# The second layer's output product by one step of Strassen's scheme, with its operand through DRAM

## The chip, the cores and the metric

The kernel runs on one core of a Trainium2 chip. The metric is the device time of one execution in microseconds; the median of several runs counts. Beside the runs there is one profiled execution with a trace of every instruction. The engines are TensorE (PE, with its weight loads as PEld), VectorE (DVE), ScalarE (ACT), GpSimd (POOL) and SyncE (SP), whose queue issues all DMAs here.

## The reference

A causal attention with a cumulative bias, then two feed-forward layers. What is touched is the second layer:

```python
def _moe2_ref(x, w_in, w_out):          # x (2304, 512), w_in (512, 2048), w_out (2048, 512)
    h = x @ w_in
    g = h - np.tanh(h)
    return (g @ w_out).astype(np.float32)
```

The weights come as float64 and the products have to be as exact as float32.

## The kernel before

Each operand of a product is held as two float32r parts, a high part `h` and the rest `l`, and each product is three matmuls: high by high, high by low, low by high. ScalarE makes the high part by a copy, VectorE or GpSimd the low one by a subtraction. Weights arrive as float64 words and pass through `Conversion`: a DMA of 512 KB, one ScalarE operation, three VectorE operations on 512 words (lines 88, 89, 91), a ScalarE copy and a GpSimd subtraction.

The stages follow each other: attention with the gate and value products of the first layer (matmuls of 256 and 320 columns at lines 347, 348, 351), the first layer's output product (lines 540 to 559, blocks of 384 tokens), then the second layer. The order on each engine is the order in which the code issues, and SP's queue takes its DMAs in that order too; a DMA whose buffer isn't free holds up those behind it.

The second layer runs over 6 blocks of 384 tokens and, in each, over 16 pieces m of 128 columns of the hidden width. `hmm` makes the tanh product of one (block, m): 12 matmuls of 384 columns into one of two banks (lines 581, 582, 585), then tanh on ScalarE, the subtraction, the copy to the high part and the subtraction of the low part. `outp` adds the piece's share of the output: 9 matmuls of 512 columns (line 605), three token tiles by three parts, into three banks that stay open over the 16 pieces. `outp` of a pair is issued behind `hmm` of the next, so that the tanh chain has a tanh product's time. In the first block the output weights are still being converted, by POOL among others. At the end of a block ScalarE and VectorE copy the three banks out and SP stores them. `ysplit` makes the two parts of the layer's input y, four copies and four subtractions for a block.

## Time and profile before

| | us |
|---|---|
| median of 3 runs | 1157.69 (1157.55 to 1158.14) |
| profiled execution, span | 1156.5 |
| of it: TensorE busy | 1063.0 |
| VectorE busy | 724.9 |
| ScalarE busy | 539.2 |
| GpSimd busy | 391.1 |
| matmuls | 6501 |

The span is the time from the first to the last instruction of the profiled execution; the time of a run has about a microsecond around it. The shares of the span mean little here, since the attention stage is shared among all engines while the two output products and the second layer are not. One has to read the stages apart: the view of stretches gives the busy time of each engine in each, the timeline the distance between instructions, the groups by shape the mean length of an operation. A matmul's printed length contains its way through the array; how many fit into a microsecond is told by start times alone.

### The profile page before, as it was taken

The page shows a single profiled execution, that of the slowest core. Times are in us where ns is not written, and L with a number is a line of the kernel's source. Part 1 is how long each engine was busy: PE and PEld are TensorE (multiplying, and loading weights), DVE is VectorE, ACT ScalarE, POOL GpSimd, SP SyncE. Part 2 cuts the span into 40 slices and gives each one's busy share as a digit, 9 for nine tenths or more (in the row PEclk, how much of TensorE's full clock was granted, in tenths as well). Part 3 has the DMA queues.
Part 4 walks back from the last instruction along what each step waited for, and adds up shares of the span by engine and source line. Part 5 has one row for each costly group of instructions (what it writes and reads, how often), then busy time and mean ns, then how long its engine had stood idle before and what let it go on. Part 6 is the DMA issues. An engine that isn't in the chain of part 4 may idle for free.

```text
span 1156.5 us, 18998 instructions
## 1 busy us (share of the span) xinstructions
PE 1063.0 (92%) x6501; PEld 997.0 (86%) x6501; DVE 724.9 (63%) x1783; ACT 539.2 (47%) x1325; POOL 391.1 (34%) x524
## 2 busy tenths in 40 slices
PE   3457799989999999999899999999999999999998
PEld 2346699989899899898889999997899999999997
DVE  7999967688878788873856677378423233232322
ACT  4565556566666666653434444344323232232322
POOL 6786645466656566651311222023000000000000
PEclk9999999999999999999999999999999999999999
DMA  6556444443433433321746655233000000000000
GB/s 190 163 161 176 115 119 127 135 144 114 132 120 124 120 125 120 119 77 40 231 146 180 185 167 172 71 96 106 28 1 28 1 22 6 1 28 1 28 1 28
DMA packets 64417, 114.11 MB, mean 99 GB/s; under 512 B 7168, under 2 KB 40960, under 8 KB 64320
## 3 DMA queue, kind: packets, MB, share of 16 engines
q1 hardware_dynamic: 64320, 112.90, 31.8%
q8 instruction: 51, 0.84, 0.3%
q14 instruction: 46, 0.38, 0.1%
HBM read 93.92 MB, written 18.95 MB: 98 GB/s over the span
## 4 chain that ended last, share of the span: by engine, by line
PE 72%; DVE 15%; issue 5%; DMA 3%; ACT 3%; SPq 0%; POOL 0%; DVEq 0%; ACTq 0%; POOLq 0%
PE bank L605 15%; PE bank L348 6%; PE bank L347 6%; PE bank L351 6%; PE bank L581 5%; PE bank L582 5%; PE bank L585 5%; PE bank L300 4%; DVE raw L89 4%; PE bank L548 4%; PE bank L549 4%; PE bank L552 4%; PE bank L273 4%; PE bank L223 2%; DMA raw<-in_wo 2%
## 5 line engine op out<-in xcount | busy, mean ns | idle before, releaser
L588 DVE TENSOR_TENSOR th<-bank,th 128x384 f32<-128x384 f32 x96 | 53.5, 557 | 196.2 <-ACT th L587 196.1
L273 PE MATMUL bank<-ident,sp 128*128 128x128 f32 (+1 forms) x480 | 78.6, 273 | 68.8 <-DVE ptl L287 35.2
L286 ACT ACTIVATE pth<-bank 128x320 fp32r<-128x320 f32 (+2 forms) x160 | 69.6, 435 | 146.8 <-PE bank L300 88.1
L587 ACT ACTIVATE th<-bank 128x384 f32<-128x384 f32 x96 | 46.9, 488 | 192.0 <-PE bank L585 192.0
L273 PEld LDWEIGHTS bank<-ident,sp 128*128 128x128 f32 (+1 forms) x480 | 51.8, 143 | 86.6 <-DVE ptl L287 37.7
L243 ACT ACTIVATE sp<-sp,nm 128x576 f32<-128x576 f32 (+2 forms) x160 | 95.9, 599 | 45.0 <-DVE nm L236 44.8
L287 DVE TENSOR_TENSOR ptl<-bank,pth 128x320 fp32r<-128x320 f32 (+2 forms) x160 | 77.6, 485 | 49.0 <-ACT pth L286 33.0
L206 POOL TENSOR_SCALAR_AFFINE_SELECT nb<-nb 128x128 f32<-128x128 f32 x160 | 48.0, 300 | 150.9 <-DVE nb L205 115.1
L592 DVE TENSOR_TENSOR g2l<-th,g2h 128x384 fp32r<-128x384 f32 x96 | 53.6, 558 | 56.7 <-ACT g2h L591 56.7
L591 ACT ACTIVATE g2h<-th 128x384 fp32r<-128x384 f32 x96 | 50.4, 525 | 62.4 <-DVE th L588 62.4
L205 DVE TENSOR_SCALAR nb<-cbc,cumn 128x576 f32<-128x576 f32 (+2 forms) x160 | 76.6, 479 | 2.2 <-DMA cbc<-cum 2.2
L236 DVE CUSTOM_DVE_ANT_0 sp<-bank,nb 128x288 f32<-128x288 f32 (+2 forms) x160 | 75.6, 472 | 1.2 <-POOL nb L206 0.2
L223 PE MATMUL bank<-kh,qs 128*128 128x384 f32 (+1 forms) x192 | 70.7, 373 | 6.0 <-POOL qs L172 6.0
L89 DVE SCALAR_TENSOR_TENSOR raw<-raw 128x512 uint32<-128x512 uint32 x68 | 74.2, 1091 | 2.3
L496 DVE TENSOR_TENSOR gl<-g,gh 128x384 fp32r<-128x384 f32 x72 | 39.6, 556 | 57.3 <-PE bank L552 38.1
L261 DVE TENSOR_SCALAR sp<-sp,r 128x128 f32<-128x128 f32 (+1 forms) x96 | 72.6, 756 | 3.4
L168 POOL TENSOR_TENSOR kl<-kq,kh 128x256 fp32r<-128x256 f32 (+1 forms) x64 | 73.0, 1141 | 3.6 <-ACT kh L167 2.8
L300 PE MATMUL bank<-pth,vs 128*128 128x256 f32 (+1 forms) x224 | 71.2, 335 | 0.6 <-ACT pth L286 0.6
L495 ACT ACTIVATE gh<-g 128x384 fp32r<-128x384 f32 x72 | 37.1, 526 | 71.2 <-PE bank L549 60.8
L96 ACT ACTIVATE tmp<-raw 128x512 f32<-128x512 f32 x68 | 45.5, 669 | 46.6 <-DMA raw<-in_wo 26.8
L300 PE MATMUL bank<-ptl,vs 128*128 128x256 f32 (+1 forms) x224 | 64.7, 309 | 0.1
L91 DVE SCALAR_TENSOR_TENSOR tmp<-tmp,raw 128x512 uint32<-128x512 uint32 x68 | 59.9, 881 | 6.0 <-DVE raw L89 0.5
(588 smaller groups left out, 3405.3 us busy)
## 6 DMA issues: line engine op xcount, KB each, us to landing
kq<-in_kq SPq DMA_DIRECT2D x32, 448.0 KB, 3.6
raw<-in_wo SPq DMA_DIRECT2D x28, 512.0 KB, 3.6
g<-g SPq DMA_DIRECT2D x72, 192.0 KB, 3.4
cbc<-cum SPq DMA_DIRECT2D x32, 288.0 KB, 4.0
kq<-in_kq SPq DMA_DIRECT2D x32, 256.0 KB, 3.5
raw<-in_win SPq DMA_DIRECT2D x16, 512.0 KB, 3.6
g<-gt SPq DMA_DIRECT2D x48, 160.0 KB, 1.8
raw<-in_wg SPq DMA_DIRECT2D x12, 512.0 KB, 4.4
```

What stands on the lines that cost most here:

```text
L89: DVE.scalar_tensor_tensor(out=lo, in0=lo, scalar=29, in1=hi, op0=ALU.logical_shift_right, op1=ALU.bitwise_or)
L168: POOL.tensor_tensor(out=kl, in0=d["k"], in1=kh.bitcast(F), op=ALU.subtract)
L205: DVE.tensor_scalar(out=n, in0=c, scalar1=cumn[:, t, j:j + 1], scalar2=0.0, op0=ALU.add, op1=ALU.min)
L223: PE.matmul(ps, d["qs"][:, o:o + 128], d["kh"][:, c0:c1], start=True, stop=False)
L236: DVE.tensor_tensor_reduce(out=sp[:, c0:c1], in0=ps[:, 0:c1 - c0], in1=e["nb"][:, c0:c1], scale=-0.125, scalar=init, op0=ALU.add, op1=ALU. ...
L243: ACT.activation(out=e["sp"], in_=e["sp"], func=AF.Exp, scale=-1.0, bias=e["m"], accum_out=e["sum"])
L261: DVE.tensor_scalar(out=e["sp"], in0=e["sp"], scalar1=e["r"], scalar2=None, op0=ALU.mult)
L273: PE.transpose(ps[:, j, :], e["sp"][p0:128, c:c + 128], ident[p0:128, p0:128])
L286: ACT.activation(out=ph[:, js, o:o + n], in_=e["tr"], func=AF.Copy)
L287: DVE.tensor_tensor(out=pl[:, js, o:o + n], in0=e["tr"], in1=ph[:, js, o:o + n].bitcast(F), op=ALU.subtract)
L300: PE.matmul(ps[:, o:qw], d["vs"][:, j].rearrange("p a d -> p (a d)"), p[:, slot, o:qw], start=(n == 0 and m == 0), stop=(n == len(jobs) - ...
L605: PE.matmul(acc[t], g[:, t * 128:t * 128 + 128], w, start=(m == 0 and k == 0), stop=(m == M2 - 1 and k == 2))
```

## The change

The second layer falls into two stages. In the first, `hmm` runs alone, over 8 blocks of 288 tokens by 16 pieces (128 units), into eight banks in turn; each unit's g, h minus tanh(h) in float32, is stored to DRAM (`g2scr`). In the second, the output product is made from four quarters of g (token halves by halves of the hidden width) and four quarters of the output weights, by seven products in place of eight (Strassen's scheme in Winograd's form).

The seven weight operands of a pair p of pieces (p and p + 8) are made during the first stage by `PairConversion`: two 512 KB loads, the conversion as before, four GpSimd sums of 256 columns, two ScalarE copies and two GpSimd subtractions for the two parts. Pairs 0 to 2 stay in SBUF; pairs 3 to 7 are stored to DRAM (`w2scr`, 1.84 MB each) and come back over the place of the input weights (`wload`): 3 and 4 in the last block, 5 to 7 in the first steps of the second stage.

The second stage runs over five passes s of tokens (four of 256 in each half, one of 128) and in each over the 8 pairs p; (s, p) is called a step here. `sload` loads the four quarters' pieces of g (0.52 MB, three DMAs, two buffers); `sprep` makes three of the seven operands by a copy and four by sums: two on POOL, two on VectorE, then two ScalarE copies (768 and 1024 elements) for the high and two VectorE subtractions for the low parts, into buffers that are used in turn by every second step. A step has 42 matmuls of 256 columns, in the short pass 21, into seven banks, one for each product. In the last step of a pass `drain` copies product 1 out by ScalarE and adds the others on VectorE, seven additions, and four stores leave. The first layer's stage loses three conversions (from 19 to 16), and the pools are laid out anew. The diff, cut; the conversion's arithmetic is moved into two functions and unchanged:

```diff
+MP = M2 // 2
+ND = 3
+HBLK = 288
+NHB = NT // HBLK
+TB = 256
+DG = 2
+NSB = -(-(NT // 2) // TB)
+OG = {1: 0, 2: 1, 3: 6, 4: 2, 5: 3, 6: 4, 7: 5}
+OW = {1: 2, 2: 0, 3: 1, 4: 6, 5: 3, 6: 4, 7: 5}
+OORD = (1, 2, 6, 7, 5, 4, 3)
...
+    class PairConversion:
...
+            yield start
+            yield second
+            yield join(0)
+            yield join(1)
+            yield self.keep
+            for a in todo[:2]:
+                yield add(*a)
+            yield lambda: self.load(p + 1)
+            yield high(*cuts[0])
+            for a in todo[2:]:
+                yield add(*a)
+            yield low(*cuts[0], False)
+            yield high(*cuts[1])
+            yield low(*cuts[1], True)
...
-        if blk < NBLK:
+        if blk < NHB:
...
-        ps = bank(i % 2, [128, BLK])
+        ps = bank(i % 8, [128, HBLK])
...
-        th = fp.tile([128, BLK], F, tag="th2", name="th2")
+        th = fp.tile([128, HBLK], F, tag="th2", name="th2", bufs=6)
         ACT.activation(out=th, in_=ps, func=AF.Tanh)
         DVE.tensor_tensor(out=th, in0=ps, in1=th, op=ALU.subtract)
-        gh = fp.tile([128, BLK], R, tag="g2h", name="g2h")
-        gl = fp.tile([128, BLK], R, tag="g2l", name="g2l")
-        ACT.activation(out=gh, in_=th, func=AF.Copy)
-        DVE.tensor_tensor(out=gl, in0=th, in1=gh.bitcast(F), op=ALU.subtract)
-        G2[i] = gh, gl
-
-    def outp(i):
...
-    for blk in range(NBLK):
-        hmm(blk * M2)
-        for m in range(M2):
-            if blk == 0:
+        SP.dma_start(out=g2scr[m][:, blk * HBLK:(blk + 1) * HBLK], in_=th)
...
+    def sprep():
...
+        POOL.tensor_tensor(out=t[:, 0], in0=a21, in1=a22, op=ALU.add)
+        DVE.tensor_tensor(out=t[:, 2], in0=a11, in1=a21, op=ALU.subtract)
+        POOL.tensor_tensor(out=t[:, 1], in0=t[:, 0], in1=a11, op=ALU.subtract)
+        ACT.activation(out=sh[:, 0:3], in_=g[:, 1:4], func=AF.Copy)
+        DVE.tensor_tensor(out=t[:, 3], in0=a12, in1=t[:, 1], op=ALU.subtract)
+        DVE.tensor_tensor(out=sl[:, 0:3], in0=g[:, 1:4], in1=sh[:, 0:3].bitcast(F), op=ALU.subtract)
+        ACT.activation(out=sh[:, 3:7], in_=t, func=AF.Copy)
+        DVE.tensor_tensor(out=sl[:, 3:7], in0=t, in1=sh[:, 3:7].bitcast(F), op=ALU.subtract)
+        sload(i + DG)
+        S_["s", i] = sh, sl
...
+        hmm(i)
+        if m == M2 // 2:
+            ysplit(blk + 1)
...
+        if i == len(order) - 8 or i == len(order) - 4:
+            sprep()
+        if blk == NHB - 1:
+            if m in (6, 10):
+                wload(ND + (m == 10))
...
+        for n in OORD:
+            g, f = OG[n], OW[n]
+            for t in range(nt):
...
+                PE.matmul(o, sh[:, g, c], w[:, 0, f], start=(p == 0 and t == 0), stop=False)
+                PE.matmul(o, sh[:, g, c], w[:, 1, f], start=False, stop=False)
+                PE.matmul(o, sl[:, g, c], w[:, 0, f], start=False, stop=(p == MP - 1 and t == nt - 1))
+            if p == MP - 1:
+                drain(s, n, nt * 256)
+        sprep()
+        if i + ND + 2 < MP:
+            wload(i + ND + 2)
```

On TensorE, before, within a block of the second layer: the end of one `hmm`, then `outp` of the pair before it (names: `wb` output weights, `wi` input weights, `yh` and `yl` the parts of y, `g2h` the high part of g).

```order
L581 MATMUL bank_11621<-yh,wi8h 128x384
L582 MATMUL bank_11621<-yh,wi8l 128x384
L585 MATMUL bank_11621<-yl,wi8h 128x384 x4
L605 MATMUL bank_11435<-wb7h,g2h 128x512
L605 MATMUL bank_11435<-wb7l,g2h 128x512
L605 MATMUL bank_11436<-wb7h,g2h 128x512
L605 MATMUL bank_11436<-wb7l,g2h 128x512
L605 MATMUL bank_11437<-wb7h,g2h 128x512
L605 MATMUL bank_11437<-wb7l,g2h 128x512
```

And now, TensorE where the first stage ends and the second begins (`big` holds the input weights, `wo` the output weights' seven operands).

```order
L707 MATMUL bank_13226<-yh,big_9213 128x288
L708 MATMUL bank_13226<-yh,big_9213 128x288
L711 MATMUL bank_13226<-yl,big_9213 128x288 x4
L841 MATMUL bank_13246<-wo_10724,sh 128x256
L842 MATMUL bank_13246<-wo_10724,sh 128x256
L843 MATMUL bank_13246<-wo_10724,sl 128x256
L841 MATMUL bank_13246<-wo_10724,sh 128x256
L842 MATMUL bank_13246<-wo_10724,sh 128x256
L843 MATMUL bank_13246<-wo_10724,sl 128x256
L841 MATMUL bank_13247<-wo_10724,sh 128x256
```

All output matmuls have moved behind the last tanh product, and they are narrower: three parts for each of two token tiles, bank by bank.

On VectorE, before, at the end of a block: a copy of one output bank stands among the tanh subtractions.

```order
L588 TENSOR_TENSOR th_11345<-bank_11332,th_11345 128x384
L592 TENSOR_TENSOR g2l<-th_11345,g2h 128x384
L537 TENSOR_TENSOR yl<-y,yh 128x384
L610 COPY o<-bank_10833 128x512
L588 TENSOR_TENSOR th_11408<-bank_11395,th_11408 128x384
L592 TENSOR_TENSOR g2l<-th_11408,g2h 128x384
```

And now, VectorE at the last step of the fourth pass (`s` the sums, `g` what was loaded, `sl` the low parts, `o` the output; in brackets the engines and DMAs that each waits for).

```order
L752 TENSOR_TENSOR s_15092<-g_14989 128x128 [waits DMAHW5_49,DMAHW4_49]
L755 TENSOR_TENSOR s_15092<-g_14989,s_15092 128x128 [waits DMAHW6_49,Pool_49]
L756 TENSOR_TENSOR sl<-g_14989,sh 128x3x128 [waits PE_49,Activation_49]
L758 TENSOR_TENSOR sl<-s_15092,sh 128x4x128 [waits Activation_49]
L798 TENSOR_TENSOR o<-bank_14702,o 128x512 [waits PE_49,Activation_49]
L798 TENSOR_TENSOR o<-bank_14703,o 128x512 [waits PE_49]
L798 TENSOR_TENSOR o<-bank_14704,o 128x512 [waits DVE_49,PE_49]
L798 TENSOR_TENSOR o<-bank_14705,o 128x512 [waits DVE_49,PE_49]
L798 TENSOR_TENSOR o<-bank_14705,o 128x512
L798 TENSOR_TENSOR o<-bank_14706,o 128x512 [waits PE_49]
L798 TENSOR_TENSOR o<-bank_14707,o 128x512 [waits DVE_49,PE_49]
L752 TENSOR_TENSOR s_15169<-g_15046 128x128 [waits DMAHW7_49,DMAHW0_49]
```

The seven additions stand between the operand work for two steps, and the later one is queued behind them.

On SP, before, the second layer has the last raw weight loads and then only the stores of the output, `L69 DMA raw<-in_wo` 13 times and `L614 DMA out<-o` 18 times. And now, SP from the last store of the first stage on (`h` is g in DRAM, `w` the weight operands there).

```order
L715 DMA h_94<-th_13239 128x288
L738 DMA g_13306<-h_83 128x256 x2
L738 DMA g_13306<-h_91 128x2x256
L764 DMA wo_13310<-w_100 128x3584
L738 DMA g_13365<-h_84 128x256 x2
L738 DMA g_13365<-h_92 128x2x256
L764 DMA wo_13369<-w_101 128x3584
L738 DMA g_13424<-h_85 128x256 x2
L738 DMA g_13424<-h_93 128x2x256
L764 DMA wo_13428<-w_102 128x3584
```

Each weight load stands behind a load of g, which waits for its buffer, and between two such loads.

## Rows read from the trace of the kernel before

**Rows 1.** Stretches: busy us per engine (instructions), clock, DMA share, GB/s.

```profile
640.00:746.00 106.00, 106.00 (x613) 106.00 (x612) 67.08 (x95) 47.50 (x96) 19.21 (x15) 1.00 0.47 144
815.00:1087.00 272.00, 272.00 (x1363) 245.71 (x1362) 84.07 (x154) 78.41 (x158) 0.00 (x0) 1.00 0.04 13
```

**Rows 2.** Timeline, TensorE, first pair: start us, length us, line, tiles, count.

```profile
746.72 0.34 PE L581 MATMUL bank<-yh,wi0h 128*128 128x384 f32 x1
...
748.11 0.85 PE L585 MATMUL bank<-yl,wi0h 128*128 128x384 f32 x4
```

**Rows 3.** Timeline of TensorE, one (block, m) pair of the second layer.

```profile
902.95 0.34 PE L581 MATMUL bank<-yh,wi5h 128*128 128x384 f32 x1
...
904.37 0.86 PE L585 MATMUL bank<-yl,wi5h 128*128 128x384 f32 x4
905.06 0.40 PE L605 MATMUL bank<-wb4h,g2h 128*128 128x512 f32 x1
...
907.15 0.34 PE L581 MATMUL bank<-yh,wi6h 128*128 128x384 f32 x1
```

**Rows 4.** Timeline of the end: span, last matmul, last copy of the output.

```profile
core 0 of [0], span 1156.5 us
...
1152.46 0.39 PE L605 MATMUL bank<-wb15h,g2l 128*128 128x512 f32 x1
1152.88 0.60 ACT L612 ACTIVATE o<-bank 128x512 f32<-128x512 f32 x1 [0.79 <-PE bank L605]
```

**Rows 5.** Timeline of TensorE, attention stage: a run of 256 columns.

```profile
199.80 0.28 PE L347 MATMUL bank<-xh,w02h 128*128 128x256 f32 x1
...
200.52 0.64 PE L351 MATMUL bank<-xl,w02h 128*128 128x256 f32 x4
```

**Rows 6.** The same, a run of 320 columns.

```profile
584.43 0.31 PE L347 MATMUL bank<-xh,w09h 128*128 128x320 f32 x1
...
585.46 0.31 PE L348 MATMUL bank<-xh,w09l 128*128 128x320 f32 x1
```

**Rows 7.** Groups by shape, ScalarE: count, busy us, mean ns, idle before.

```profile
L167 ACT ACTIVATE kh<-kq 128x576 fp32r<-128x576 f32 x32 | 21.6, 676 | 0.0
...
L167 ACT ACTIVATE kh<-kq 128x256 fp32r<-128x256 f32 x32 | 12.9, 404 | 9.3 <-DMA kq<-in_kq 9.3
```

**Rows 8.** Groups by shape, VectorE (DVE) and GpSimd (POOL).

```profile
L592 DVE TENSOR_TENSOR g2l<-th,g2h 128x384 fp32r<-128x384 f32 x96 | 53.6, 558 | 56.7 <-ACT g2h L591 56.7
...
L287 DVE TENSOR_TENSOR ptl<-bank,pth 128x512 fp32r<-128x512 f32 x32 | 22.1, 690 | 19.8 <-ACT pth L286 19.3
L363 DVE SCALAR_TENSOR_TENSOR gt<-th,bank 128x256 f32<-128x256 f32 x48 | 19.9, 414 | 11.9 <-ACT vs L185 5.3 <-ACT kh L167 3.2 <-ACT th L360 2.9
...
L168 POOL TENSOR_TENSOR kl<-kq,kh 128x256 fp32r<-128x256 f32 x32 | 26.7, 834 | 2.8 <-ACT kh L167 2.8
...
L186 POOL TENSOR_TENSOR vs<-vraw,vs 128x128 fp32r<-128x128 f32 x32 | 16.0, 499 | 8.5 <-ACT vs L185 7.5 <-DMA cbc<-cum 0.4
```

**Rows 9.** Timeline, VectorE and POOL: conversions without and beside POOL work.

```profile
563.54 0.69 DVE L89 SCALAR_TENSOR_TENSOR raw<-raw 128x512 uint32<-128x512 uint32 x1
...
790.15 0.42 DVE L88 TENSOR_SCALAR raw<-raw 128x512 uint32<-128x512 uint32 x1
...
790.25 1.48 POOL L83 TENSOR_TENSOR wb10l<-tmp,wb10h 128x512 fp32r<-128x512 f32 x1 [3.54 <-DVE g2l L592]
...
790.61 1.67 DVE L89 SCALAR_TENSOR_TENSOR raw<-raw 128x512 uint32<-128x512 uint32 x1
...
792.38 0.69 DVE L91 SCALAR_TENSOR_TENSOR tmp<-tmp,raw 128x512 uint32<-128x512 uint32 x1
```

**Rows 10.** Stretches (DMA share, GB/s last); DMA issues: count, KB, median landing.

```profile
96.00:100.00 4.00, 3.55 (x30) 3.55 (x31) 3.86 (x7) 1.98 (x6) 2.94 (x3) 1.00 0.97 368
700.00:704.00 4.00, 4.00 (x25) 4.00 (x24) 2.69 (x3) 2.13 (x4) 1.33 (x1) 1.00 0.78 263
...
raw<-in_wo SPq DMA_DIRECT2D x28, 512.0 KB, 3.6
```

More of the change, by code (lines that the diff above doesn't have):

```diff
@@ L592, in hmm @@
-        DVE.tensor_tensor(out=gl, in0=th, in1=gh.bitcast(F), op=ALU.subtract)
-        G2[i] = gh, gl
-    def outp(i):
-        blk, m = order[i]
-        if m == 0:
-            acc[:] = [bank(2 + 3 * (blk % 2) + t, [128, DM]) for t in range(3)]
-        gh, gl = G2.pop(i)
-        wh, wl = wo2n[m]
-        parts = ((gh, wh), (gh, wl), (gl, wh))
-        end = i == len(order) - 1
-        for t, k in sorted(((t, k) for t in range(3) for k in range(3)), key=lambda x: x if end else (x[1] == 2, x)):
-            g, w = parts[k]
-            PE.matmul(acc[t], g[:, t * 128:t * 128 + 128], w, start=(m == 0 and k == 0), stop=(m == M2 - 1 and k == 2))
-        if m == M2 - 1:
-            for t in range(3):
-                o = fp.tile([128, DM], F, tag="o", name="o", bufs=3)
-                if t == 1:
-                    DVE.tensor_copy(out=o, in_=acc[t])
-                else:
-                    ACT.activation(out=o, in_=acc[t], func=AF.Copy)
-                r0 = blk * BLK + t * 128
-                SP.dma_start(out=out[r0:r0 + 128, :], in_=o)
@@ new lines, in d_open, with sload @@
+    def d_open():
+        y_left.close()
+        DP["g"] = ctx.enter_context(tc.tile_pool(name="dg", bufs=2, side="left"))
+        DP["s"] = ctx.enter_context(tc.tile_pool(name="ds", bufs=2, side="right"))
+        for i in range(DG):
+            sload(i)
+    def sload(i):
+        if i >= NSB * MP:
+            return
+        s, p = divmod(i, MP)
+        tb = dwidth(s)
+        g = S_["g", i] = DP["g"].tile([128, 4, TB], F, tag="g2", name="g2", bufs=DG)
+        for f, (m, t0) in enumerate(((p, NT // 2), (p, 0), (p + MP, 0), (p + MP, NT // 2))):
+            if f == 3:
+                continue
+            k = 2 if f == 2 else 1
+            src = g2scr[m].rearrange("p (a t) -> p a t", a=2)[:, t0 // (NT // 2):t0 // (NT // 2) + k, s * TB:s * TB + tb]
+            SP.dma_start(out=g[:, f:f + k, 0:tb], in_=src)
@@ new lines, in wload @@
+    def wload(p):
+        WO[p] = w2.tile([128, 2, 7, 256], R, tag=f"w{p - ND}", name=f"wo2{p}")
+        SP.dma_start(out=WO[p].bitcast(F), in_=w2scr[p])
+    cvt = PairConversion(cv4, [("right", [wo2[m * 128:(m + 1) * 128].bitcast(U) for m in (p, p + MP)], p)
+                               for p in range(MP)], dst, POOL)
+    n0, n1 = 4, len(order) - M2 - 4
+    for i, (blk, m) in enumerate(order):
+        hmm(i)
+        if m == M2 // 2:
+            ysplit(blk + 1)
+        if n0 <= i < n1:
+            for _ in range((i + 1 - n0) * len(cvt.steps) // (n1 - n0) - (i - n0) * len(cvt.steps) // (n1 - n0)):
+                cvt.tick()
+        if i == n1:
+            cvt.finish(MP - 1)
+            cvt.keep()
+            c_right.close()
+        if i == len(order) - M2 - 2:
+            d_open()
+        if i == len(order) - 8 or i == len(order) - 4:
[3 more added lines that the diff above has]
+                wload(ND + (m == 10))
@@ new lines, in attention_moe_moe2, with otile, dadd, ostore @@
+    dsteps = [(s, p) for s in range(NSB) for p in range(MP)]
+    op = ctx.enter_context(tc.tile_pool(name="op", bufs=1, side="left"))
+    acc = {}
+    def otile(k, w):
+        return op.tile([128, 512], F, tag=k, name="o")[:, 0:w]
+    def dadd(k, x, y, w, op=ALU.add):
+        o = otile(k, w)
+        DVE.tensor_tensor(out=o, in0=x, in1=y, op=op)
+        return o
+    def ostore(s, lo_tok, half, o, w):
+        r0 = (0 if lo_tok else NT // 2) + s * TB
+        SP.dma_start(out=out[r0:r0 + w // 2, half * 256:half * 256 + 256].rearrange("(a p) c -> p a c", p=128),
+                     in_=o.rearrange("p (a c) -> p a c", c=256))
```

166 lines of the change are left out of this document (140 added, 26 removed).

## The prediction, made before the changed kernel ran

> **What bounds the kernel now.** I read the stretches first. From 640 to 746 us (first layer's output product) and from 815 to 1087 us (second layer) TensorE is busy in every microsecond at granted clock 1.00, while in the second stretch VectorE is busy for 84 of 272 us, ScalarE for 78 and GpSimd for none [rows 1]. So the second layer costs the number of its matmuls times the distance from one start to the next. The printed length of a matmul is no such distance: the nine 512-column matmuls of a pair start 0.23 us apart, and each is printed with 0.40. I take distances from start times in the timeline. The layer starts at 746.72 [rows 2]. One (block, m) pair, 12 matmuls of 384 columns and 9 of 512, runs from 902.95 to 907.15, 4.20 us, of which the wide nine take 2.09 from 905.06 on, 0.232 each [rows 3]; 96 pairs make 403.2 us. The last matmul ends at 1152.46 + 0.39 = 1152.85, the span at 1156.5 [rows 4]. So 406.1 us of the layer are 403.2 of TensorE pace plus 2.9 of waiting at its two ends, and 3.65 are tail.
>
> **Up to 746.7 us: nothing.** Three conversion jobs fewer run under the first layer's output product, where TensorE was never waiting [rows 1]. I start the sum at 746.7.
>
> **The tanh product: 1536 matmuls of 288 columns in place of 1152 of 384.** 288 columns don't occur as a dense run; the nearest rows lie on both sides. 256 columns: 199.80 to 200.52, six distances, 0.120 us [rows 5]. 320 columns: 584.43 to 585.46, seven, 0.147 us [rows 6]. The middle is 0.1335, and 1536 x 0.1335 = 205.1 us. One correction: in the second layer the eight matmuls on yh run at 0.1775 each (902.95 to 904.37) [rows 3], while the first eight of the layer, before any evacuation runs beside them, took 0.174 (746.72 to 748.11) [rows 2]. That is 2% on two thirds of the matmuls, 2.7 us if it stays; I take half and put 206.6 us, bounds 205.1 and 208.4. No output product is interleaved any more, so nothing in this stage waits for a tanh chain except a bank, and there are eight: 12 x 0.1335 = 1.6 us each, 12.8 us round. Under that cover lie, for each unit, a tanh of 288 (ScalarE's copies take 0.40 at 256 and 0.68 at 576 [rows 7]), a subtraction (0.56 at 384 [rows 8]), eight splits a block, and the conversion of the output weights with its POOL sums. The longest thing put in front of a tanh or a subtraction is one conversion's three VectorE operations, 0.42 + 0.69 + 0.69 free and up to 1.67 for one of them beside POOL [rows 9]: some 5 us at worst. Without the eight banks that would be a stall at each of 16 conversions. SP's new store per unit (147 KB) and the weight stores (1.84 MB, five times) have over 160 us; raw loads stand behind them in the queue and nobody is late.
>
> **The output product: 1512 matmuls of 256 columns in place of 864 of 512.** Seven products for eight, four passes of 256 tokens (8 steps of 42 matmuls) and one of 128 (8 steps of 21): 1512 x 0.120 = 181.4 us; 0.119 and 0.122 bound it, 180 to 184.5. The columns fall by 12.5%, the time by less: 864 x 0.232 = 200.4, so 9.5%, because a narrow matmul costs more per column. In all 388.0 us against 403.2: **15.2 us gained** in TensorE's pace.
> The page "TensorE: Matmul & The Clock Gate" of the Trainium skill, section "Back-to-back issue gap", gives columns/2.4 GHz plus 2.5 ns; by it 256 columns would take 109 ns (an estimate from that page), and the change would save 20 us instead of 15. The rows above contradict it at every width by 10 ns or more, so the sum goes by the rows.
>
> **What the new stage asks of the others.** A step lasts 42 x 0.120 = 5.04 us. Its operands are made two steps ahead, in buffers that the step before last sets free, so ScalarE's and VectorE's part must fit in one step. ScalarE: 768 and 1024 elements; 256 take 0.404 and 576 take 0.676 [rows 7], 0.85 ns an element, hence 0.84 and 1.06. VectorE: two operations of 256, one of 768, one of 1024; from 0.558 at 384 with 1.09 ns an element [rows 8] 0.42, 0.42, 0.98, 1.26, together 3.08. POOL: two sums of 256 at 0.834 [rows 8], 1.67. The chain after the release is 0.84 + 1.06 + 1.26, some 3.4 with handoffs: hidden by 1.6. But POOL and VectorE get in each other's way: VectorE's operation on two SBUF inputs that takes 0.69 alone took 1.67 when it met a POOL sum, and ended 0.55 after that one [rows 9]: one ran, then the other. If that holds here they share one resource: 3.08 + 1.67 = 4.75 of 5.04. It fits, with 0.3 to spare, so for a plain step I put 0.
> The page "SBUF — State Buffer" of the Trainium skill, section "Who interferes with whom", speaks against the change here: a VectorE instruction with two SBUF inputs and a GpSimd instruction that reads SBUF exclude each other, which all the new operand work on both engines does. By that rule the sum below holds; without it the stalls would be some 2 us instead of 6.
> *Ends of passes.* VectorE adds seven products, 7 x 0.69 = 4.83 [rows 8], in one step beside its 3.08. Following the queue from the end of step 6 of a pass (time 0): its operand work ends at 3.3 (4.5 with POOL in between), the adds at 8.2 (9.4), the two differences for step 9 at 9.0 (10.3), its first low part at 10.0 (11.3). Step 9 starts at 10.1 and wants that part 0.24 later: a stall of 0 to 1.1, I take 0.6, three times: 1.8. Into the short pass it is worse, since its steps last 21 x 0.120 = 2.52: the last adds free their bank 1.1 to 2.3 too late, and step 9's low part costs 0.5: 2.2. In the short pass itself VectorE needs 0.28 x 2 + 0.56 + 0.69 = 1.81 and POOL 2 x 0.499 = 1.0 [rows 8], 2.81 against 2.52: 0.3 a step, 8 steps, 2.0 rounded down. **Stalls 6 us**, bounds 1.5 and 16 (all ends at their worst, and 0.2 for each of 40 steps).
> *Reloads.* The weights of pairs 5 to 7 (1.84 MB each) are asked for 7, 12 and 17 us into the stage, each between loads of g (0.52 MB), and wanted at 25, 30 and 35 us. The queue moved 368 GB/s where it was full [rows 10]: 5.0 + 1.4 = 6.4 us per weight and g load, the last in at 28 us. Hidden by 7 us. Pairs 3 and 4 are asked for 14 and 8 us before the stage and wanted 15 and 20 us into it: hidden by more.
>
> **The tail.** The last step leaves seven adds of 256 on VectorE, 0.41 each [rows 8], some 3.2 us with handoffs. They begin when the second product is done, five products of 0.36 before the last matmul ends, so they end 1.4 to 1.5 after it. Then a store; before, from the end of the last copy (1152.88 + 0.60) to the end were 3.0 [rows 4]. 4.5 us.
>
> **Sum.** 746.7 + 206.6 + 181.4 + 6 + 4.5 = 1145.2 us of span. The median of the runs lies 1.2 above the profiled span: **1146 us**.
>
> **Rivals.**
> *Clean.* POOL and VectorE rarely meet, and the yh correction vanishes: 205.1 and 1.5 of stalls, 1145.2 - 1.5 - 4.5, a span of 1139 and a time of 1140. For it: POOL's two sums may fall where VectorE waits for ScalarE. Against: the rows leave them 0.3 us of room a step. 0.15.
> *The loads pace the first pass.* No window shows what the queue gives beside this mix; one busy for 0.78 of the time gave 263 GB/s [rows 10]. At that rate a weight and a g load take 9 us together, the g of step 7 lands at 36.8 instead of 30, and steps 6 and 7 lose 4.5 us; at 220 GB/s some 9. 1151 to 1156. Against: the share shows that the 263 was demand. 0.12.
> *Slower: the loop of the g buffers.* The load for step j+2 is issued when the first low part of j has been taken from the same buffer; then come landing, two POOL sums, a blocked VectorE operation, a difference, the low part of j+2: landing + 0.1 + 1.67 + 1.26 + 0.42 + 0.98 = landing + 4.4, to fit in two steps, 10.1. 512 KB landed in 3.6 [rows 10], so it fits by 2. Past 5.7 TensorE waits in every pair of steps, 16 pairs of the long passes: at 6.5 they cost 13.6 us and the kernel is at 1160, the point from which it is slower; at 6.8 us, 1165. For it: each load is three pieces in short rows, with weight traffic beside it in the first pass. Against: in the later passes there is no other load, and the queue has 5 us for 0.52 MB. 0.10.
> *The cut isn't one in time.* If 256-column matmuls with a new stationary each ran at 0.130 instead of 0.120, 15 us would go and the time would be 1161 with the stalls. Rows 5 are just such matmuls, in a busier stretch. 0.05.
>
> **How the numbers follow.** Forecast 0.55 (own range 1141 to 1151), clean 0.15, loads 0.12, loop 0.10, pitch 0.05, anything else 0.03. Faster by over 0.2% (below 1155.4; about what a measurement of this kernel can tell): forecast, clean and most of the loads, 0.81. Slower (above 1160.0): loop and some of the pitch, 0.12. Between: 0.07. Range: from half of the clean case, 1138, to the upper end of the loads, 1156; left out are the slower cases and a little below.
>
> **What would show it.** Tanh stage: a unit every 1.60 to 1.63 us, TensorE without a gap, the stage over at 953. Output stage: steps of 5.0 us in the long passes, gaps only at the second step of a pass and in the short pass, put down to VectorE's low part, and VectorE operations of twice their length beside POOL. A wait of matmuls for wo would show the loads; one for ScalarE's or VectorE's part in every step, with g landing over 5.7 us, the loop. Steps above 5.3 us without a wait would mean the pitch. The prediction is wrong if the two stages together are not 388 us of TensorE pace give or take 4, or the stalls pass 16.

## The result and the profile after

The change makes the kernel faster: 1138.09 us median (1136.91 to 1138.92) against 1157.91 for the kernel before in the same session, a ratio of 0.9828 with a 95% interval of 0.9814 to 0.9842. That is 19.8 us gained, 1.7%; 11.7 were forecast. The profiled execution has a span of 1137.1 us.

The stretches of the second layer, kernel after: first the tanh stage, then three pieces of the output stage. The columns are those of [rows 1].

```profile
748.32:951.85 203.53, 203.53 (x1538) 203.53 (x1537) 103.62 (x211) 86.50 (x195) 63.06 (x54) 1.00 0.57 199
952.00:1000.00 48.00, 48.00 (x408) 48.00 (x407) 33.67 (x45) 17.62 (x20) 15.64 (x17) 1.00 0.75 268
1000.00:1050.00 50.00, 50.00 (x422) 50.00 (x421) 40.65 (x48) 18.83 (x21) 25.15 (x22) 1.00 0.43 128
...
1111.00:1133.00 22.00, 21.88 (x173) 20.78 (x172) 15.52 (x36) 8.27 (x15) 5.94 (x12) 1.00 0.35 106
```

TensorE is busy in every microsecond at clock 1.00, as in [rows 1], up to the short pass, which starts at 1111.4. VectorE has gone up to 40.65 of 50 us and GpSimd from nothing to 25.15 of 50, and still TensorE waits for neither in the long passes. The first piece has the reloads of weights: DMA share 0.75.

The marks of the two stages in the timeline of TensorE, and the span; they answer to [rows 2] and [rows 4].

```profile
core 0 of [0], span 1137.1 us
...
748.32 0.30 PE L707 MATMUL bank<-yh,big 128*128 128x288 f32 x1
...
951.85 0.28 PE L841 MATMUL bank<-wo,sh 128*128 128x256 f32 x1
...
1132.74 0.28 PE L843 MATMUL bank<-wo,sl 128*128 128x256 f32 x1
```

The tanh stage takes 951.85 - 748.32 = 203.53 us, 0.1325 a matmul (1536 of them). The output stage takes 1132.74 - 951.85 = 180.89 from its first start to its last, 0.1197 from one start to the next (1511 distances). The last matmul ends at 1133.02, and 4.1 us follow. Beside the forecast:

| term, us | forecast | measured | difference |
|---|---|---|---|
| start of the second layer | 746.7 | 748.3 | +1.6 |
| tanh stage | 206.6 | 203.5 | -3.1 |
| output product, pace and stalls | 181.4 + 6 | 181.2 | -6.2 |
| tail | 4.5 | 4.1 | -0.4 |
| span | 1145.2 | 1137.1 | -8.1 |

The first row is no effect of the change: in the nine profiled executions that follow the change's layout the layer starts between 745.0 and 748.9, with code ahead of it that is the same or nearly so, and 746.7 lies among them.

The operand work by shape in the output stage, kernel after: count, busy us, mean ns, idle time before. They answer to [rows 7] and [rows 8].

```profile
L758 DVE TENSOR_TENSOR sl<-s,sh 128x1024 fp32r<-128x1024 f32 x31 | 44.9, 1447 | 2.8 <-ACT sh L757 2.6
L756 DVE TENSOR_TENSOR sl<-g,sh 128x768 fp32r<-128x768 f32 x30 | 29.5, 984 | 21.5 <-ACT sh L754 21.4
L752 DVE TENSOR_TENSOR s<-g 128x256 f32<-128x256 f32 x30 | 22.9, 762 | 1.0 <-DMA g<-h 1.0
...
L755 DVE TENSOR_TENSOR s<-g,s 128x256 f32<-128x256 f32 x30 | 13.0, 435 | 9.4 <-POOL s L753 9.4
...
L753 POOL TENSOR_TENSOR s<-s,g 128x256 f32<-128x256 f32 x30 | 36.4, 1214 | 2.3
L751 POOL TENSOR_TENSOR s<-g 128x256 f32<-128x256 f32 x30 | 32.2, 1074 | 93.2 <-DMA g<-h 84.6 <-DVE sl L758 5.1 <-DVE sl L756 2.8
...
L754 ACT ACTIVATE sh<-g 128x768 fp32r<-128x768 f32 x30 | 25.4, 847 | 79.4 <-PE bank L842 69.3 <-issue 5.4 <-DMA g<-h 4.5
```

VectorE and GpSimd do hold each other up: the difference of 256 takes 0.76 us on average, 0.42 where nothing meets it, and the GpSimd sums 1.07 and 1.21, where the shortest took 0.73. What matters stands behind the bars. GpSimd starts its sums when g lands (84.6 us of waiting for that), a step ahead. ScalarE's first copy waits for TensorE to set its buffer free (69.3 us), VectorE's low part waits for that copy (21.4). So the chain behind a step begins with the buffer that TensorE frees, and the sums are done by then. By this trace that is why the meeting of the two engines costs nothing here; the run `sums_dve` below tests it.

The end of the second pass, VectorE, kernel after: the adds of pass 2, then the operands of the step that starts at 1036.67.

```profile
1028.61 1.69 DVE L758 TENSOR_TENSOR sl<-s,sh 128x1024 fp32r<-128x1024 f32 x1
1030.22 4.66 DVE L798 TENSOR_TENSOR o<-bank,o 128x512 f32<-128x512 f32 x7
1034.79 0.48 DVE L752 TENSOR_TENSOR s<-g 128x256 f32<-128x256 f32 x1
1035.20 0.41 DVE L755 TENSOR_TENSOR s<-g,s 128x256 f32<-128x256 f32 x1
1035.53 0.95 DVE L756 TENSOR_TENSOR sl<-g,sh 128x768 fp32r<-128x768 f32 x1
1036.74 1.23 DVE L758 TENSOR_TENSOR sl<-s,sh 128x1024 fp32r<-128x1024 f32 x1 [0.26 <-ACT sh L757]
```

And GpSimd, the same stretch.

```profile
1033.43 0.74 POOL L751 TENSOR_TENSOR s<-g 128x256 f32<-128x256 f32 x1 [2.54 <-DMA g<-h]
1034.25 0.74 POOL L753 TENSOR_TENSOR s<-s,g 128x256 f32<-128x256 f32 x1
```

The first low part is ready at 1036.48, and the third matmul of the step, which reads it, starts at 1036.91: 0.43 us to spare. The queue goes as the prediction followed it, near the lower end of each pair of its numbers: counted from the end of step 6 (1026.65) the operand work ends at 3.7 (its last low part takes 1.69 for 1.23, with GpSimd sums beside it), the adds at 8.2, the differences at 9.0, the low part at 9.8, and the step starts at 10.0. The sums shown, which were to come in between, lie beside the adds, each of which reads one operand from a matmul's bank, and both take the free 0.74 there.

The loads of weights in the changed kernel: count, KB, median us from issue to landing, first of all five and then of the last, issued at 970.47.

```profile
wo<-w SPq DMA_DIRECT2D x5, 1792.0 KB, 8.4
...
wo<-w SPq DMA_DIRECT2D x1, 1792.0 KB, 10.0
```

From issue to landing a weight load takes 8.4 us, but several loads are under way at once: those of pairs 5 to 7 are issued at 960.4, 965.4 and 970.5 and are in at 967.6, 974.8 and 980.5, 6.45 us apart on average, where the prediction had 6.4 for a weight and a g load. The last is in 28.6 us into the stage (the prediction had 28), 6.2 before its step starts at 986.67. Tighter is the load of g that stands behind it in the queue: issued at 973.93, it is complete at 981.73, and the low part made from it was ready 1.07 us before its use. The loads of g, in pieces of 128 and 256 KB, took 5.5 and 5.6 us from 940 to 976 us, and 2.1 and 3.2 in the later passes.

### The profile page after: what moved, and what is told of

It reads as the page before. It is cut to its first block, busy times and chain, and to the rows that moved or that the text cites. A ratio compares the mean times of both kernels' runs of the same rounds, so it can differ in the third digit from the quotient of the medians.

```text
span 1137.1 us, 22118 instructions
## 1 busy us (share of the span) xinstructions
PE 1047.2 (92%) x7533; PEld 1021.6 (90%) x7533; DVE 805.7 (71%) x1916; ACT 561.9 (49%) x1342; POOL 506.7 (45%) x636
## 4 chain that ended last, share of the span: by engine, by line
PE 77%; DVE 13%; issue 5%; ACT 2%; DMA 1%; SPq 0%; POOL 0%; DVEq 0%; ACTq 0%; POOLq 0%
PE bank L466 7%; PE bank L467 7%; PE bank L470 7%; PE bank L708 6%; PE bank L711 6%; PE bank L707 6%; PE bank L843 5%; PE bank L842 5%; PE bank L841 5%; PE bank L419 4%; PE bank L670 4%; PE bank L669 4%; PE bank L673 4%; PE bank L392 4%; DVE raw L112 3%
## 5 line engine op out<-in xcount | busy, mean ns | idle before, releaser
L843 PE MATMUL bank<-wo,sl 128*128 128x256 f32 x504 | 142.7, 283 | 0.1
L841 PE MATMUL bank<-wo,sh 128*128 128x256 f32 x504 | 141.9, 282 | 0.0
L842 PE MATMUL bank<-wo,sh 128*128 128x256 f32 x504 | 141.9, 281 | 0.0
L708 PE MATMUL bank<-yh,big 128*128 128x288 f32 x512 | 139.6, 295 | 0.0
L707 PE MATMUL bank<-yh,big 128*128 128x288 f32 x512 | 139.6, 294 | 0.0
L714 DVE TENSOR_TENSOR th<-bank,th 128x288 f32<-128x288 f32 x128 | 56.2, 454 | 102.1 <-ACT th L713 102.1
L713 ACT ACTIVATE th<-bank 128x288 f32<-128x288 f32 x128 | 51.3, 410 | 95.2 <-PE bank L711 83.7
L843 PEld LDWEIGHTS bank<-wo,sl 128*128 128x128 f32 x504 | 95.3, 189 | 1.0 <-DVE sl L758 0.3
L708 PEld LDWEIGHTS bank<-yh,big 128*128 128x128 f32 x512 | 96.2, 188 | 0.0
L707 PEld LDWEIGHTS bank<-yh,big 128*128 128x128 f32 x512 | 96.0, 188 | 0.0
L842 PEld LDWEIGHTS bank<-wo,sh 128*128 128x128 f32 x504 | 95.4, 189 | 0.0
L841 PEld LDWEIGHTS bank<-wo,sh 128*128 128x128 f32 x504 | 95.4, 189 | 0.0
L751 POOL TENSOR_TENSOR s<-g 128x256 f32<-128x256 f32 (+1 forms) x40 | 37.8, 944 | 123.2 <-DMA g<-h 112.9
L711 PE MATMUL bank<-yl,big 128*128 128x288 f32 x512 | 88.7, 295 | 0.0
```

The costliest lines, as they stand in the source:

```text
L707: PE.matmul(ps, wh[:, c], Y_[blk][k][0], start=(k == 0), stop=False)
L708: PE.matmul(ps, wl[:, c], Y_[blk][k][0], start=False, stop=False)
L711: PE.matmul(ps, wh[:, c], Y_[blk][k][1], start=False, stop=(k == KD - 1))
L841: PE.matmul(o, sh[:, g, c], w[:, 0, f], start=(p == 0 and t == 0), stop=False)
L842: PE.matmul(o, sh[:, g, c], w[:, 1, f], start=False, stop=False)
L843: PE.matmul(o, sl[:, g, c], w[:, 0, f], start=False, stop=(p == MP - 1 and t == nt - 1))
```

## The experiments

**The first stage alone.** `plain` keeps the two stages and the way of g through DRAM and takes Strassen's scheme out: 864 output matmuls of 512 columns again.

```diff
-            for t in range(nt):
-                PE.matmul(o, sh[:, g, c], w[:, 0, f], start=(p == 0 and t == 0), stop=False)
...
+            PE.matmul(acc[t], g[:, t * 128:t * 128 + 128], w, start=(m == 0 and k == 0), stop=(m == M2 - 1 and k == 2))
```

> The two stages and the way of g through DRAM stay, but the output product is the plain one of the kernel before: 864 matmuls of 512 columns, g loaded in pieces of 384 tokens and split again. Theory (the gain is TensorE's pace in the output product, from the seven products): tanh stage 203 us as in the changed kernel, output stage 864 x 0.23 = 199 to 201 us, tail 3.7, so a span of 1153 to 1156; the split alone is worth 0 to 3 us and Strassen's step some 19. Rival (the gain comes from taking the two products apart, which rids TensorE of the tanh chain and of the slow pace of mixed matmuls): the 512-column matmuls run at 0.218 and the span comes to 1143 or less.

1182.75 us, a ratio of 1.0216 (1.0195 to 1.0238), which neither theory has. The output stage is clean, 201.4 us; the tanh stage takes 228.1 instead of 203.5. The waits of TensorE (us in total, times, longest) and, from the timeline of ScalarE, a tanh and the conversion behind it:

```profile
PE bank L699 <- DVE th L706: 15.8, 9, 3.5
```
```profile
802.62 0.41 ACT L705 ACTIVATE th<-bank 128x288 f32<-128x288 f32 x1 [1.75 <-DMA h<-th]
...
807.82 0.66 ACT L119 ACTIVATE tmp<-raw 128x512 f32<-128x512 f32 x1 [4.26 <-DMA raw<-in_wo]
```

ScalarE stands 4.26 us for weight words whose load was issued in the same step of the conversion, and three tanhs stand behind it. It also stands 1.75 us for the store that gives a staging buffer of the tanh result back: `plain` has three of them where the changed kernel has six, and over the stage these waits come to 40 us on ScalarE. Both are faults of this experiment's own and say nothing of the scheme. `plain2` asks for the words three units earlier, converts every fifth unit and has four staging buffers:

```diff
...
-        if i >= 4 and i % 4 == 0 and cvt.ticks < M2 + 3:
+        if i >= 5 and i % 5 == 0 and cvt.ticks < M2 + 3:
             cvt.tick()
+        if i % 5 == 2:
+            cvt.load()
```

> The two stages without Strassen's scheme again (tanh blocks of 288, g through DRAM, then 864 output matmuls of 512 columns), now with the weight words loaded two units before ScalarE takes them, and a conversion every fifth unit instead of every fourth. In the run named plain the second stage was clean (201.4 us from first to last matmul, no gap) and all the excess lay in the tanh stage (228.1 us), where ScalarE stood 3.4 to 4.3 us at a conversion's first copy, behind a load issued in the same step, with the tanhs queued behind it. Theory A (the excess is that queue and nothing else, and it is the scheme's seven eighths that make the gain of the changed kernel): the tanh stage goes back to 203.5 us; 748 + 203.5 + 201.4 + 3.5 = 1156.5 of span, a time of 1157 to 1158, no different from the kernel before. Rival B (the stores of g and the loads beside the tanh product cost too): tanh stage above 210 us, time above 1163. Rival C (part of the 19.8 us gained comes from separating the stages): time below 1154.

1158.54 us; the ratio to the kernel before is 1.0002 (0.9989 to 1.0015). The stretches of its two stages:

```profile
745.00:948.50 203.50, 203.50 (x1538) 203.50 (x1537) 108.07 (x205) 78.72 (x193) 22.21 (x16) 1.00 0.42 133
948.60:1150.00 201.40, 201.40 (x865) 161.94 (x864) 56.57 (x101) 55.08 (x106) 0.00 (x0) 1.00 0.37 112
```

The time is theory A's; which of the three changes cured the tanh stage the run does not tell, since it made them together. Separating the stages in blocks of 288 costs nothing and brings nothing: 203.5 + 201.4 = 404.9, where the mixed layer took 406.1. The gain is the output product's alone, 201.4 down to 180.9, 20.5 us, of which the forecast had 13 (200.4 less 181.4 and 6). With blocks of 384, whose tanh stage takes 199.7 (`blk384`, below), the separation by itself would be worth some 5 us, an estimate from these two stages that no run here tried.

**Do VectorE and GpSimd limit a step?** `six` leaves out product 3, and with it a part of the output: a step has 36 matmuls and the operand work stays. `pool2x` makes each GpSimd sum twice.

```diff
-OORD = (1, 2, 6, 7, 5, 4, 3)
+OORD = (1, 2, 6, 7, 5, 4)
...
```
```diff
         POOL.tensor_tensor(out=t[:, 0], in0=a21, in1=a22, op=ALU.add)
+        POOL.tensor_tensor(out=t[:, 0], in0=a21, in1=a22, op=ALU.add)
...
```

> Product 3 of the seven is left out, so one output quarter is not the reference's; all loads, sums and parts are still made. Theory (TensorE's pace sets the long passes, the rest is hidden): 1296 matmuls at 0.1197 are 155.1 us, so the long passes fall by 22 to 23 us to about 138, in steps of 4.3; the short pass falls by less than 3, since its loop of the g buffers already sets it. Rival (POOL and VectorE exclude each other, 4.5 to 4.75 us of work a step, as the prediction has it): steps stop at 4.5 to 4.75, and the long passes stay at 144 to 152 us.

> Each of POOL's two sums per step is made twice. Theory of the prediction (POOL and VectorE share one resource, 3.0 us of VectorE and now 3.0 to 3.3 of POOL in a step of 5.0): 6.0 to 6.4 us a step, the output stage longer by 30 to 45 us. Rival (they slow each other only where they happen to meet, and each fits by itself): no more than 5 us longer, POOL busy 3 us a step beside VectorE.

These two runs, `six_nr` and `sums_dve` were timed once each.

`six`: 1127.37 us, span 1125.6, only 11.5 less than the kernel after for 216 matmuls that take 25.9. The long passes take 145.4 us, 4.5 a step, where the theory had 138: by the total alone the rival's floor of 4.5 to 4.75 us a step, the sum of both engines' work, would look right. The steps say otherwise. Starts of steps in the timeline of TensorE, `six`, the last two steps of the first pass and one plain step of the fourth, and what TensorE waited for:

```profile
978.00 0.28 PE L842 MATMUL bank<-wo,sh 128*128 128x256 f32 x1
...
984.00 0.28 PE L842 MATMUL bank<-wo,sh 128*128 128x256 f32 x1
...
992.20 0.28 PE L842 MATMUL bank<-wo,sh 128*128 128x256 f32 x1
...
1085.13 0.28 PE L842 MATMUL bank<-wo,sh 128*128 128x256 f32 x1
...
1089.35 0.28 PE L842 MATMUL bank<-wo,sh 128*128 128x256 f32 x1
```
```profile
PE bank L844 <- DVE sl L756: 6.5, 8, 2.1
```

The plain step takes 4.22 us, 36 x 0.117: there is no floor at 4.75. The time is lost in places: 6.00 and 8.20 at the end of the first pass, 4.9 to 5.3 in one or two steps at the start of each later pass (4.3 without a stall), and in the short pass, 2.1 to 3.6 where 2.1 would be enough.

`pool2x`: 1156.6 us, span 1154.8, 18.5 and 17.7 more than after. Here too the first steps keep their length, 5.02, 5.04, 5.04, 4.93, 4.93, with GpSimd at twice its work. Later ones alternate, 4.9 to 5.2 and 5.7 to 6.0 in the third and fourth passes, and the two at the start of a pass take 5.9 to 6.7. What TensorE waited for in it, and GpSimd's part in VectorE's idle time:

```profile
PE bank L845 <- DVE sl L758: 9.6, 13, 1.7
...
L757 DVE TENSOR_TENSOR s<-g,s 128x256 f32<-128x256 f32 x30 | 17.6, 586 | 34.6 <-POOL s L755 34.6
```

(L757 here is what L755 is in the kernel after.) The wait of the difference for GpSimd goes from 9.4 to 34.6 us. One round of the loop, in the fourth pass, VectorE and GpSimd:

```profile
1100.63 0.94 DVE L758 TENSOR_TENSOR sl<-g,sh 128x768 fp32r<-128x768 f32 x1
...
1111.04 0.41 DVE L757 TENSOR_TENSOR s<-g,s 128x256 f32<-128x256 f32 x1
1111.38 0.94 DVE L758 TENSOR_TENSOR sl<-g,sh 128x768 fp32r<-128x768 f32 x1
```
```profile
1106.13 0.74 POOL L751 TENSOR_TENSOR s<-g 128x256 f32<-128x256 f32 x1
...
1109.24 1.59 POOL L755 TENSOR_TENSOR s<-s,g 128x256 f32<-128x256 f32 x1
```

The low part that ends at 1101.57 frees a buffer of g; load, four sums, a difference and a low part later, at 1112.32, the next but one is made: 10.75 us for two steps, and two steps at TensorE's pace are 10.0. That is the loop of the g buffers, the prediction's slower rival, closed by the sums instead of the landing. The four sums take 4.70 us in it, from 1106.13 to 1110.83, where four of 0.74 are 3.0: here the meeting of the two engines lies on the chain, and it costs. In the kernel after the same loop takes some 9 us. Nor do the engines' printed times add up: 3.02 us of VectorE and 4 x 0.74 of GpSimd, each at its free length, are 6.0 a step, and the eleven steps of the third and fourth passes behind their first two took 5.3 on average (the last step of the fourth left aside). So the theory that both engines' lengths add up falls in both runs, and so does the rival that expected nearly nothing of `pool2x`. What costs in them are chains that had some 0.4 to 1.1 us of room in the kernel after: the ends of passes (0.43), the loads of the first pass (1.07) and the loop of the g buffers (some 1).

**The reloads.** `six_nr` is `six` without the reloads of weights 5 to 7.

```diff
         if i + ND + 2 < MP:
-            wload(i + ND + 2)
+            WO[i + ND + 2] = WO[i + ND - 1]
```

> As the run named six (product 3 left out, so a part of the output is wrong), and also without the reload of the weights of pairs 5 to 7: these pairs use the weights of pairs 2, 3 and 4 instead. In six the last two steps of the first pass took 6.0 and 8.2 us against 4.22 in plain steps. Theory A (those 5.8 us are loads of g that stand behind three weight loads of 1792 KB): both steps fall to about 4.25, the span from 1125.6 to about 1120; the starts of later passes (4.9 for 4.3, twice a pass) and the short pass stay as they were. Rival B (the first pass is slow because VectorE and GpSimd hold each other up there): the two steps stay at 6 and 8, the span stays at 1125.

1121.58 us, span 1119.8, 5.8 less. The stretch of the two steps in `six` and then in `six_nr`, each with the stretch ahead of it:

```profile
952.50:978.00 25.50, 25.50 (x217) 25.50 (x216) 13.94 (x20) 8.56 (x10) 6.86 (x9) 1.00 0.94 354
978.00:992.00 14.00, 10.46 (x73) 10.05 (x72) 10.42 (x14) 5.25 (x6) 4.64 (x7) 0.88 0.46 143
```
```profile
952.50:978.00 25.50, 25.50 (x217) 25.50 (x216) 19.59 (x23) 9.32 (x12) 11.45 (x10) 1.00 0.55 168
978.00:992.00 14.00, 13.18 (x110) 12.85 (x110) 12.82 (x17) 5.79 (x8) 6.40 (x6) 1.00 0.54 168
```

With the reloads the DMA engines are full (0.94, 354 GB/s) up to 978, and TensorE then stands for 3.5 of 14 us. The granted clock of these 14 us is 0.88, which adds to the loss. In `six`, TensorE alone:

```profile
987.30:990.60 3.30, 3.30 (x18) 0.51 0.64 182
```

At 0.51, the lower of the two levels (1.2 GHz), the matmuls are 0.21 us apart instead of 0.117, some 1.5 us for sixteen; before that TensorE had stood for 1.4 and 2.1 us. Without the reloads the two steps take 4.23 and 4.22 at a clock of 1.00; the 0.8 us left in that stretch is the start of the next pass, which comes earlier now. So the loads do pace the first pass as soon as a step is 0.7 us shorter. In the kernel after they lie just under it.

**GpSimd's sums on VectorE.**

```diff
-        POOL.tensor_tensor(out=t[:, 0], in0=a21, in1=a22, op=ALU.add)
+        DVE.tensor_tensor(out=t[:, 0], in0=a21, in1=a22, op=ALU.add)
...
```

> The two sums of 256 columns that GpSimd makes in each step go to VectorE, which never meets GpSimd then. Theory A (the meeting of both costs no time in the changed kernel, since GpSimd makes its sums a step ahead of the point at which the operand buffers come free): the difference of VectorE by line 752 falls from 0.8 to 0.42 us and the low part of 1024 from 1.47 to 1.23, VectorE has two operations of 0.42 more, long steps stay at 4.92 to 5.04, and at the ends of passes, where the low parts were 0.4 us early, the later step loses 0.4 to 0.8 us three or four times; the short pass, whose loop holds two sums of 0.46 on GpSimd, gains some 0.3 us in every second step; span 1136 to 1139. Rival B (the meeting lengthens the operand chain and the tail): the short pass falls to 2.55 a step and the span by 1.5 us or more.

1137.18 us in one run, span 1135.4 with a layer that starts 1.5 earlier: from the start of the layer to the end 388.6 us, after 388.8. The lengths went as theory A has it, 0.418 for 0.762 at line 752 and, below, 1.225 for 1.447:

```profile
L758 DVE TENSOR_TENSOR sl<-s,sh 128x1024 fp32r<-128x1024 f32 x31 | 38.0, 1225 | 2.9 <-ACT sh L757 2.8
```

The steps at the starts of passes lost less than expected (5.12 to 5.14 for 5.04, three times), the short pass has two stalls of 0.5 and 0.9 and is otherwise at 2.5. It is a draw: the meeting of the two engines, with all its lengthened operations, costs the kernel after nothing that this run can tell. (The steps of pairs 3 to 7 run at 4.93 in all four long passes of it, where the kernel after has 4.98 in two: 0.5 us, of which the starts of passes take 0.3 back.)

**Tanh blocks of 384 and the best version.** `blk384` sets the tanh stage back to 1152 matmuls of 384 columns (with three staging buffers for the tanh result, and one buffer fewer in two other places, for room).

```diff
-HBLK = 288
+HBLK = 384
...
```

> Tanh product in 6 blocks of 384 columns instead of 8 of 288, nothing else changed but buffer counts. If the 0.177 us of the yh matmuls in the kernel before came from the evacuation running beside them (the prediction's correction), it is here again and the stage takes 768 x 0.177 + 384 x 0.1735 = 202.6 us, the time is that of the changed kernel within 1. If it came from the mixing with the 512-column matmuls, all run at 0.1735 and the stage takes 199.9, 3.5 us less, and the kernel comes to 1134.

1135.6 us (1132.72 to 1137.13), a ratio of 0.9809 (0.9781 to 0.9837). The stage in its timeline:

```profile
746.90 0.34 PE L707 MATMUL bank<-yh,big 128*128 128x384 f32 x1
...
946.59 0.28 PE L841 MATMUL bank<-wo,sh 128*128 128x256 f32 x1
```

199.7 us, 0.1733 a matmul, for all twelve of a unit. That is the pace of [rows 2], and the 0.1775 of [rows 3] is gone with the output matmuls in between. The output stage begins with a stall of 0.94, where a tanh waited for a store to give its staging buffer back.

`best` takes the 384, five staging buffers for the last units, three buffers for g instead of two, and each output buffer once.

```diff
-DG = 2
+DG = 3
...
+        if "t" in DP and i % 5 > 2:
+            th = DP["t"].tile([128, HBLK], F, tag="th3", name="th2", bufs=2)
```

> Tanh blocks of 384 as in the run named blk384, five staging buffers for g at the end of the tanh stage instead of three, three buffers instead of two for the loads of g, and each output buffer once instead of twice to make room. Theory A (three separate terms that add): tanh product at 0.1733 us a matmul, 1152 x 0.1733 = 199.7 us for 203.5, so 3.9 less; the 0.94 us gap at the start of the second stage in blk384, a tanh that waited for a store with its buffer, goes; the loop of the short pass (landing, two sums on GpSimd, a difference, a low part, over two steps) has three steps instead of two, and its excess over 2.51 us a step, 1.3 us, goes. Span 1137.1 - 3.9 - 1.3 = about 1132, or 1129 from a start of the layer at 746 to 747; time 1131 to 1134. Rival B (VectorE and GpSimd together are the limit in the short pass, 2.8 us a step): the short pass stays at 2.6 to 2.7 a step, time 1134 to 1136. Rival C (each output buffer has to wait for its store): gaps at the ends of passes.

1132.96 us (1131.0 to 1133.53), a ratio of 0.9773 (0.9758 to 0.9787) to the kernel before: 5 us better than the kernel after, 25 better than before. Its stretches (tanh stage, short pass):

```profile
747.19:946.88 199.69, 199.69 (x1154) 199.69 (x1154) 96.52 (x171) 81.71 (x155) 63.49 (x56) 1.00 0.59 210
...
1106.46:1126.22 19.76, 19.76 (x169) 19.76 (x168) 15.56 (x34) 8.04 (x15) 6.20 (x10) 1.00 0.31 95
```

TensorE never stands in the whole layer (in the long passes it is busy for 159.58 of 159.58 us). The short pass takes 19.9 us (2.46 to 2.52 a step) where the kernel after has 21.4 (2.46 to 3.07) and `blk384`, with two buffers for g as well, 22.1, with the same work on VectorE and GpSimd. So it was the loop through two buffers, and rival B falls. One round of it in the kernel after, a GpSimd sum and the difference of VectorE that waits for the sums:

```profile
1117.54 0.46 POOL L751 TENSOR_TENSOR s<-g 128x128 f32<-128x128 f32 x1 [5.35 <-DMA g<-h]
...
1118.58 0.29 DVE L755 TENSOR_TENSOR s<-g,s 128x128 f32<-128x128 f32 x1 [1.66 <-POOL s L753]
```

From the low part that frees the buffer (1114.00) to the next but one (1119.34) it takes 5.34 us, and two steps at TensorE's pace are 5.0. At free lengths the two engines have 1.80 + 0.92 = 2.72 us in each of these steps of 2.47.

## Why the prediction was right or wrong, point by point

**Direction and bound: right. The step that failed most is the stalls.** TensorE bounds the layer throughout, but for 1.5 us in the short pass, the output stage runs at the pace of narrow matmuls, and no rival that ends slower took place. The time was off by 7.9 us, in three terms (and 1.6 the other way in the start of the layer). The largest is the 6 us of stalls: the prediction took VectorE and GpSimd for one shared resource and added their lengths (4.75 of 5.04 us in a step, 2.81 against 2.52 in the short pass), where the runs show 1.5 us, none of it from that sum. The other two are paces. The prediction had named a sign for them, 388 us of TensorE pace in both stages give or take 4, and 383 were measured (203.5 and, from `best`, 179.5). The nearest case is the one called clean, 1140, but that is its number and not its reason: its condition, that the two engines rarely meet, does not hold (0.76 us for 0.42); they meet where nothing waits for it.

**Up to 746.7: right** within the spread of the runs. The three conversions fewer changed nothing that shows.

**The tanh product: 3.1 us too long.** Of it 1.6 is the middle between 0.120 and 0.147, where 0.1325 was measured for 0.1335: 1536 times a thousandth. The other 1.5 is the correction, and that step failed: it carried the 0.1775 of [rows 3] over to a stage in which no output matmul is mixed in, because evacuation runs beside it there too. Evacuation runs all through `blk384`, and its matmuls take 0.1733. The trace of the kernel before had this already. In its second block, `hmm` for m = 1 comes right behind another `hmm`, with a tanh and a subtraction beside it, and its eight matmuls on yh take 0.173 each:

```profile
819.05 0.34 PE L581 MATMUL bank<-yh,wi1h 128*128 128x384 f32 x1
...
820.43 0.34 PE L585 MATMUL bank<-yl,wi1h 128*128 128x384 f32 x1
```

So evacuation it is not. Nor is it the mixed order alone, or the place of the operands: for m = 12, behind output matmuls each time and with weights and y in the same buffers, the eight take 0.173 each in the first block (796.34 to 797.72) and 0.177 in the third (932.35 to 933.77). What it is stays open. The cover of eight banks held: no gap in 203.5 us, with stores, reloads and conversions beside.

**The output product's pace: 2.0 us too long.** 1512 x 0.120 = 181.4; `best`, which has no stalls, takes 179.3 from first to last start, 0.1187. That is 0.7 below the lower bound of 180. The 0.120 of [rows 5] is the pace of the steps of pairs 0 to 2 alone (5.04 for 42); the others run at 0.117 to 0.119 (last section).
By the formula of the page "TensorE: Matmul & The Clock Gate" of the Trainium skill, section "Back-to-back issue gap", which the page gives for an isolated matmul, 256 columns would take 109 ns (an estimate from that page). Here 118.7 is measured, so the trace still disagrees with it by 10 ns.

**Stalls: 1.5 us where 6 were put, the largest error** (180.89 less the 179.34 of `best`). Three places were priced. *Ends of passes*, 1.8 and 2.2: none in the long passes, 0.2 in the second step of the short one. The chain was followed rightly, and nearly its lower value came out, with 0.4 us to spare; the failing step was to set GpSimd's sums into the middle of VectorE's chain, 1.2 us. GpSimd has a queue of its own and starts when g lands, so one step's sums stretch the operand work by some 0.4 us and the next step's run beside the adds. *The short pass*, 2.0: 1.5 measured, but for another reason. The prediction divided a sum of two engines' work by a step; `best` shows that the sum is no limit there, and that two buffers are. *A plain step*, 0: right. Its reason, that 4.75 fits into 5.04, was not needed.
The page "SBUF — State Buffer" of the Trainium skill, section "Who interferes with whom", has VectorE with two SBUF inputs and GpSimd exclude each other; the operations do lengthen, 0.42 to 0.76 and 0.74 to 1.2, which agrees in kind. It also agrees that the adds, with one input in SBUF, leave the GpSimd sums at 0.74. Taken as a sum of printed lengths that has to fit into a step, as the prediction took it, it fails in `pool2x` (6.0 in 5.3 us) and in the short pass of `best` (2.72 in 2.47); how much of an operation's printed length is exclusive, no run here shows.

**Reloads: hidden, as forecast, and by nearly as much.** The last weights were in 28.6 us into the stage, 6.2 before their use, where the prediction had 28 and 7. What it left out of this term is the load of g for the last step of the first pass, behind those weights: it landed at 29.9 us (the rival of the loads has 30 for it), and sums, difference and low part follow, so that 1.07 us were left. It cost nothing in the change. In `six`, with steps 0.7 us shorter, 5.8 us go with it, so a chance of 0.12 for the loads was not too much.

**The tail: right**, 4.1 for 4.5.

**The loop of the g buffers**, named as the slower rival: its form was right and its price was not reached, since in the later passes the pieces of a load landed in 2 to 3 us. In the first pass a whole load of g took 4.3 to 8.1 us, at times past the 5.7 of the prediction; the low parts were some 3 us early by then, and 1.07 of it was left at the last step. The loop decides the short pass, and `pool2x`.

## What to carry to other kernels

Work on a second engine counts on the chain from the event that releases it: sums that can start when data land, a step ahead of the buffer that TensorE frees, add nothing to a step even where both engines slow each other down, as long as their chain has room (in `pool2x` it had none), so follow each queue from its own release before you add two engines' times. The room that is left lies in loops through a small number of buffers. Here a third buffer took the stalls of the short pass away (`best`), and moving GpSimd's sums to the faster VectorE did not (`sums_dve`). When an experiment's total fits a theory, look at the lengths of its steps before you believe it: `six` had the total of a floor and no floor.
